# A two-branch attention with a two-layer projection on one core: the first batch in one pass of two streams, weight staging moved, loads by halves

## The chip, the cores and the metric

The kernel runs on one core of a Trainium2 chip. The metric is device time in microseconds (us) of one execution; smaller is better. The core has TensorE (matmuls; PE in the profile, its weight loads PEld), VectorE (DVE), ScalarE (ACT), GpSimd (POOL) and SyncE (SP), whose queue issues all DMAs of this kernel. Each engine works through its own queue in order; semaphores tie them together.

## The reference

```
q, k, v: [8 batches, 8 heads, 576, 64] f32
q_d, k_d, v_d = means over groups of 4 positions            # 144 positions
out_up  = repeat(softmax(q_d k_d^T / 8) v_d, 4)             # each row 4 times
out_loc = softmax(q k^T / 8 where |i - j| < 4) v            # 7 keys a row
x = out_up + out_loc, as [4608 tokens, 512]
h = x @ w_in                                                # [4608, 2048]
out = max(0.01 h, h) @ w_out                                # [4608, 512]
```

The weights `w_in` [512, 2048] and `w_out` [2048, 512] arrive as 64-bit floats; on the chip their bits are turned into a high and a low 32-bit part.

## The kernel before

*Projection.* The tokens are columns. They are cut into chunks of columns; for a chunk of n columns and each of 16 slices f of the hidden width, TensorE does 12 matmuls into a bank `hp` (`up_proj`, L698: 4 slices c of the input times 3 terms, high x high, high x low, low x high), ScalarE and VectorE make `gh` and `gl` out of it (`leaky`, L708 to L711), and TensorE does 12 matmuls into four banks `acc` (`down_proj`, L738: 4 slices e of the output, 3 terms). `store` copies the banks out.

*Chunks and passes.* Batch 0 is two chunks, 256 and 320 columns. They go through the first 8 slices f each, then through the last 8 each (`PASSES`). The partial result of the first half is written to the output in DRAM, fetched back (`refetch`) and added (L763). The other seven batches are cut into 63 blocks of 64 columns; `SIZES` groups these into chunks of 4, 5 and nine times 6 blocks. Inside a chunk a segment is up to 4 blocks of one batch.

*Batch 0* makes its local attention with matmuls on 64-row windows (`banded`, L453 to L521), in two halves of 256 and 320 columns; the averaged branch is `pooled` (L338 to L407), one call for each of four pairs of heads c. `L514` adds both, L519 and L521 split the sum into `xh` and `xl`, the input of the projection.

*The other batches* make the averaged branch with `pooled` too. In it VectorE sums q and k by fours (L338), TensorE multiplies (L351: for each third of the queries one 64-row matmul per head of the pair), softmax follows, the result is transposed (L390), multiplied with the summed v (L380, L402) and copied (L407). The local branch goes over GpSimd: `scores` multiplies q by its 7 neighbouring k (L560), VectorE sums (L566); `values` multiplies by v (L621), VectorE sums (L627); `landing` transposes the result on TensorE (L658), adds the repeated averages (L665) and splits it (L671, L673). The loads of q, k and v hold both heads of a pair, one buffer each.

*Weights.* `convert(f, k)` loads a raw slice of `w_in` (k = 0) or `w_out` (k = 1), 524 KB, into a staging place, converts it with one operation of ScalarE (L266), one of VectorE (L268), one copy (L276 or L279) and one subtraction on GpSimd (L281), and frees the place. Staging places are the buffers k, v, two `prod`, `up`, and for f < 4 also `xh1` and `xl1`. Slices f >= 9 have their final places in memory that is free only when the start's pool `su` is closed (`swap`, signal "late").

*Order.* All this is written as generators that ask a planner, `Order`, for buffers and for engine time. Each has a rank (batch 0: 1 to 5 and its second half 21; weights 20 + 2f + k; other batches from 98 up). The planner keeps a clock for each engine with estimated costs (`COST`), always takes the operation that can start first (then the lowest rank), and so fixes each engine's instruction order before the run. Its estimates give no times here; they only make the order.

Of the kernel before, what the change touches and what calls it, by code (L numbers as in the profile page):

```python
# [27 lines left out]
MAXSEG = 4  # L28
SIZES = (4, 5, 6, 6, 6, 6, 6, 6, 6, 6, 6)
# [4 lines left out]
BLKS = ((0, 4), (4, 9))  # L34
HALFS = 4
HEADS = 2
HF = NF // 2
# [3 lines left out]
def plan():  # L41

    chunks, at = [(0, 256, ()), (256, 320, ())], S
    parts = {b: [] for b in range(BANDED, B)}
    g = 0
    for i, n in enumerate(SIZES):
        mine, z = [], g + n
        while g < z:
            b, j = divmod(g, BLK)
            room = min(BLK - j, z - g)  # L50
            m = -(-room // -(-room // MAXSEG))
            mine.append((b + BANDED, j, j + m, (g - z + n) * NBLK))
            parts[b + BANDED].append((i + 2, j, j + m, (g - z + n) * NBLK))
            g += m
        chunks.append((at, n * NBLK, tuple(mine)))
        at += n * NBLK
    assert g == (B - BANDED) * BLK
    return chunks, parts
# [3 lines left out]
PASSES = [(0, 0, HF), (1, 0, HF), (0, HF, NF), (1, HF, NF)] + [(i, 0, NF) for i in range(2, len(CHUNKS))]  # L62
# [9 lines left out]
LANDED = [NC, NC] + [2 * sum(len(pieces(a, z)) for _, a, z, _ in c[2]) for c in CHUNKS[2:]]  # L72
XMAX = [max(c[1] for c in CHUNKS[i::2]) for i in range(2)]
OMAX = max(XMAX)
COST = {"ACT": (0.13, 0.00083), "DVE": (0.08, 0.00104), "POOL": (0.25, 0.00217)}
HOP = 0.2
SAFE = 0.4
# [18 lines left out]
class Order:  # L96
# [51 lines left out]
    def run(self):  # L148
        while self.tasks:
# [5 lines left out]
            else:  # L155
                best = None
                for task in self.tasks:
                    if task[3][0] == "op":
# [4 lines left out]
                        key = (start, task[0], task[1])  # L163
                        if best is None or key < best[0]:
                            best = key, task
                assert best is not None, [t[3] for t in self.tasks]
# [14 lines left out]
def attn_moe(ctx: ExitStack, tc, qkt, vd, qb, kb, vb, vwb, band, identb, w_in, w_out, ident, edge, out):  # L181
# [5 lines left out]

    bufs = dict(head=HEADS, qk=1, vs=1, qk_d=2, v_d=1, su_vd=2, su_half=1, st_d=2, pd=2, ptd=1, outd=2, q=1, k=1, v=1, s=3, st_l=3, prod=2, up=1,
                xloc=2, lst=3, gh=3, gl=3, o=2, hp=2, pt=2, xh0=1, xl0=1, xh1=1, xl1=1, acc0=1, acc1=1, acc2=1, acc3=1,
# [34 lines left out]
    w_in_v = w_in.rearrange("(c p) (f m) -> p f c m", p=128, m=128 * HALFS)  # L224
    w_out_v = w_out.rearrange("(f p) e -> p f e", p=128)

# [12 lines left out]
    def weight_tiles(pool, f0, f1):  # L239
        shape = [128, f1 - f0, NC, 128]  # L240
        wts.append((f0, *(pool.tile(shape, F32R, name=f"{nm}_{f0}") for nm in ("wih", "wil", "woh", "wol"))))

    def weight(f, k):
        f0, *ts = max((w for w in wts if w[0] <= f), key=lambda w: w[0])
        return ts[2 * k][:, f - f0], ts[2 * k + 1][:, f - f0]

    weight_tiles(const, 0, FSPLIT)

# [3 lines left out]

    def convert(f, k):
        s = yield from slot("k", "v", "prod", "up", *(("xh1", "xl1") if f < 4 else ()))
        st = sb(s, [128, HALFS * (DM + 1)], U16)
        raw = st[:, 1:1 + HALFS * DM]
        if k == 0:
            t = yield from load(raw.rearrange("p (c m) -> p c m", c=NC), w_in_v[:, f], 524e3, s.t)
        else:
            t = yield from load(raw, w_out_v[:, f], 524e3, s.t)  # L260
        mid = st.bitcast(I32).rearrange("p (m w) -> p m w", w=2)[:, :DM, 1]
        top = st.rearrange("p (m h) -> p m h", h=HALFS)[:, 1:, 0].bitcast(BF16)
        s_u = yield from slot("head")
        head = heads[s_u.index % len(heads)]
        t = yield from op("ACT", 1500, t, s_u.t)
# [5 lines left out]
        if f >= FSPLIT:  # L271
            yield from wait("late")
        hi, lo = (w.rearrange("p c m -> p (c m)") for w in weight(f, k))
# [8 lines left out]
        s.free(t)  # L282
        od.signal(("w", f, k), t)
# [12 lines left out]
    def x_tile(i):  # L296
        if i > 1:
            yield from wait(("xbuf", i - 1))
        elif i:
            yield from wait(("scored", 0, NC - 1))  # L300
        s_h, s_l = (yield from slot(f"xh{i % 2}")), (yield from slot(f"xl{i % 2}"))
        xt[i] = [sb(t, [128, NC, XMAX[i % 2]], F32R)[:, :, :CHUNKS[i][1]] for t in (s_h, s_l)]
        od.signal(("xbuf", i), max(s_h.t, s_l.t))
        t = yield from wait(("done", i), 2 if i < 2 else 1)
        s_h.free(t)
        s_l.free(t)

    def fetch(b, c, pool):
        if pool is None:
            sq, sv = (yield from slot(*(("qk", "up") if b < BANDED else ("qk",)))), (yield from slot("vs"))  # L310
            qk, vs = sb(sq, [128, 2, S], F32), sb(sv, [72, 2, 2, D, FAC], F32)
        else:
            sq, sv = None, (yield from slot("su_vs"))
            qk = pool.tile([128, 2, S], F32, name=f"qk{c}")
            vs = sb(sv, [72, 2, 2, D, FAC], F32, pool)
# [4 lines left out]
        tv = yield from load(vs, vd[b, c], 295e3, sv.t if sv else 0.0)  # L320
        return sq, sv, qk, vs, tq, tv

    def pooled(b, c, rank, pool=None):
        sq, sv, qk, vs, tq, tv = yield from fetch(b, c, pool)
        s_qd = yield from slot("qk_d")
        qk_d = sb(s_qd, [128, 2 * SD], F32)
        qkr = qk.rearrange("p a (s r) -> p (a s) r", r=FAC)
        if b < BANDED and (b, c) != (0, 0):
            s = yield from slot("su_half")
            half = sb(s, [128, 2 * SD, 2], F32, pool)  # L330
# [550 lines left out]
```

## Time and profile before

| what | value |
|---|---|
| runs | 976.35, 972.04, 976.05 us; median 976.05 |
| profiled execution | span 965.5 us from first to last instruction; its own total time is not given apart |
| TensorE busy | 936.8 us (97%), 6282 matmuls |
| GpSimd, VectorE, ScalarE busy | 611.5, 594.7, 415.6 us |
| moved by DMA | 117.31 MB, mean 122 GB/s |

In rows of the profile, "out<-in" names tiles by the program's names, "xN" counts instructions, and what stands in brackets or after the bar is the idle time of the engine ahead of them and what ended it. A row of a timeline begins with start and length in us. A stretch row gives the busy time of each engine in it with the number of instructions, then the granted TensorE clock as a share of full speed, the DMA share and GB/s. A row of waits gives the total, the number of times and the longest.

### The profile page before, as it was taken

Reading aid. Unit: us, or ns where it says so; the run is one execution under the profiler, and the core shown is the slowest. Engines: PE = TensorE matmul, PEld = TensorE weight load, DVE = VectorE, ACT = ScalarE, POOL = GpSimd, SP = SyncE. Lnnn points to the kernel's source line nnn. Section 1 sums busy time; section 2 is a strip of 40 time slices with the busy share of each in tenths; the row PEclk is TensorE's granted clock in tenths of the full one; section 3 lists DMA queues with packets and bytes.
Section 4 is the critical chain, followed back from the end, with each engine's and each line's share of the span. In section 5 each row is a group of like instructions: output and inputs, shape, how many; then the busy total and the mean of one; then the engine's idle time right before and its main releaser. Section 6 shows DMA issues by size and latency. Waiting matters only on the chain.

```text
span 965.5 us, 16163 instructions
## 1 busy us (share of the span) xinstructions
PE 936.8 (97%) x6282; PEld 897.8 (93%) x6282; DVE 594.7 (62%) x895; ACT 415.6 (43%) x1139; POOL 611.5 (63%) x356
## 2 busy tenths in 40 slices
PE   6699999899999999999999999999999999999997
PEld 4499999799999999999999899999999999999997
DVE  5897778767876786687667883872753752411111
ACT  3777655434634454345524552532422423422211
POOL 3655766777989788897889785884685783200000
PEclk9689999999999999999999999999999999999999
DMA  9857656434542543446233542351233221000000
GB/s 261 249 189 238 211 175 196 145 121 136 191 128 87 187 141 105 128 152 188 91 115 115 189 150 96 98 154 60 75 90 99 91 62 46 34 1 1 33 1 33
DMA packets 63180, 117.31 MB, mean 122 GB/s; under 512 B 4944, under 2 KB 32848, under 8 KB 63104
## 3 DMA queue, kind: packets, MB, share of 16 engines
q1 hardware_dynamic: 63104, 116.29, 38.6%
q8 instruction: 49, 0.80, 0.3%
q14 instruction: 27, 0.22, 0.1%
HBM read 105.65 MB, written 10.62 MB: 120 GB/s over the span
## 4 chain that ended last, share of the span: by engine, by line
PE 79%; DMA 8%; POOL 7%; DVE 3%; issue 2%; SPq 1%; ACT 0%; POOLq 0%; DVEq 0%; ACTq 0%
PE hp L698 36%; PE acc L738 35%; POOL prod L560 4%; DMA k<-in_kb_dram 3%; POOL prod L621 2%; PE pt L351 2%; DMA qk<-in_qkt_dram 2%; PE pt L390 2%; PE pt L402 1%; DMA v<-in_w_out_dram 1%; PE pt L658 1%; DMA out_dram<-o 1%; DMA su_vw<-in_vwb_dram 1%; DVE s L566 1%; DMA v<-in_vb_dram 1%
## 5 line engine op out<-in xcount | busy, mean ns | idle before, releaser
L560 POOL TENSOR_TENSOR prod<-q,k 128x1344 f32<-128x1344 f32 (+1 forms) x88 | 260.2, 2958 | 93.3 <-DMA k<-in_kb_dram 61.4
L698 PE MATMUL hp<-xh,wih 128*128 128x384 f32 (+2 forms) x832 | 278.7, 335 | 5.1 <-DVE gl L711 5.0
L621 POOL TENSOR_TENSOR prod<-v,s 128x1344 f32<-128x1344 f32 (+1 forms) x88 | 265.3, 3017 | 25.4 <-DVE xloc L627 16.0
L738 PE MATMUL acc<-gh,woh 128*128 128x384 f32 (+2 forms) x832 | 274.8, 330 | 0.6 <-DVE o L763 0.2
L698 PE MATMUL hp<-xl,wih 128*128 128x384 f32 (+2 forms) x832 | 269.5, 324 | 0.0
L698 PE MATMUL hp<-xh,wil 128*128 128x384 f32 (+2 forms) x832 | 269.4, 324 | 0.0
L738 PE MATMUL acc<-gh,wol 128*128 128x384 f32 (+2 forms) x832 | 269.4, 324 | 0.0
L738 PE MATMUL acc<-gl,woh 128*128 128x384 f32 (+2 forms) x832 | 269.4, 324 | 0.0
L708 ACT ACTIVATE gh<-hp 128x384 fp32r<-128x384 f32 (+2 forms) x208 | 97.3, 468 | 318.2 <-PE acc L738 303.6
L711 DVE TENSOR_TENSOR gl<-hp,gh 128x384 fp32r<-128x384 f32 (+2 forms) x208 | 108.3, 522 | 200.4 <-ACT hp L709 198.3
L698 PEld LDWEIGHTS hp<-xh,wih 128*128 128x128 f32 x832 | 157.1, 189 | 13.6 <-DVE gl L711 7.0
L738 PEld LDWEIGHTS acc<-gh,woh 128*128 128x128 f32 x832 | 156.3, 188 | 3.8 <-issue 2.2
L698 PEld LDWEIGHTS hp<-xl,wih 128*128 128x128 f32 x832 | 157.3, 189 | 0.0
L698 PEld LDWEIGHTS hp<-xh,wil 128*128 128x128 f32 x832 | 157.0, 189 | 0.0
L738 PEld LDWEIGHTS acc<-gl,woh 128*128 128x128 f32 x832 | 156.5, 188 | 0.0
L738 PEld LDWEIGHTS acc<-gh,wol 128*128 128x128 f32 x832 | 156.2, 188 | 0.0
L566 DVE TENSOR_REDUCE s<-prod 128x21 f32<-128x1344 f32 (+1 forms) x88 | 130.5, 1483 | 33.1 <-POOL prod L560 33.0
L627 DVE TENSOR_REDUCE xloc<-prod 128x192 f32<-128x1344 f32 (+1 forms) x88 | 130.3, 1481 | 30.1 <-POOL prod L621 29.8
L709 ACT ACTIVATE hp<-hp 128x384 f32<-128x384 f32 (+2 forms) x208 | 96.4, 463 | 0.0
L665 DVE TENSOR_TENSOR pt<-pt,up 128x384 f32<-128x384 f32 (+1 forms) x44 | 38.1, 865 | 31.7 <-PE pt L658 29.0
L645 ACT COPY up<-outd 128x576 f32<-128x576 f32 x84 | 52.3, 675 | 0.0
L338 DVE TENSOR_REDUCE qk_d<-qk 128x288 f32<-128x1152 f32 x29 | 39.0, 1346 | 13.6 <-DMA qk<-in_qkt_dram 13.6
(111 smaller groups left out, 748.9 us busy)
## 6 DMA issues: line engine op xcount, KB each, us to landing
k<-in_kb_dram SPq DMA_DIRECT2D x38, 576.0 KB
v<-in_vb_dram SPq DMA_DIRECT2D x38, 576.0 KB
qk<-in_qkt_dram SPq DMA_DIRECT2D x32, 576.0 KB
vs<-in_vd_dram SPq DMA_DIRECT2D x28, 288.0 KB
q<-in_qb_dram SPq DMA_DIRECT2D x38, 192.0 KB
out_dram<-o SPq DMA_DIRECT2D x36, 192.0 KB
prod<-in_w_out_dram SPq DMA_DIRECT2D x8, 512.0 KB
k<-in_w_in_dram SPq DMA_DIRECT2D x4, 512.0 KB
```

The source lines that it names most:

```text
L338: nc.vector.tensor_reduce(out=qk_d, in_=qkr, axis=AX.X, op=ALU.add)
L560: nc.gpsimd.tensor_tensor(out=prv, in0=q[:, p, a - j0:z - j0].unsqueeze(2).to_broadcast([128, n, W, D]), in1=view(k[:, p], (a - j0) * D, [ ...
L566: nc.vector.tensor_reduce(out=s[:, p, a - j0:z - j0], in_=prv, axis=AX.X, op=ALU.add)
L621: nc.gpsimd.tensor_tensor(out=prv, in0=view(v[:, p], a - j0, [[1, n], [nv, D], [1, W]]), in1=s[:, p, a - j0:z - j0].unsqueeze(2).to_broadc ...
L627: nc.vector.tensor_reduce(out=xl_t[:, :n, p], in_=prv, axis=AX.X, op=ALU.add)
L645: nc.scalar.copy(out=up[:, pp], in_=outd[b][:, 2 * u + pp].unsqueeze(2).to_broadcast([128, SD, FAC]))
L665: nc.vector.tensor_tensor(out=xv, in0=xv, in1=upv, op=ALU.add)
L698: nc.tensor.matmul(hp[:, :n], wt[:, c], x[:, c], start=k == 0, stop=k == 3 * NC - 1)
L708: nc.scalar.activation(out=gh[:, :n], in_=hp[:, :n], func=AF.Prelu, alpha=0.01)
L709: nc.scalar.activation(out=hp[:, :n], in_=hp[:, :n], func=AF.Prelu, alpha=0.01)
L711: nc.vector.tensor_tensor(out=gl[:, :n], in0=hp[:, :n], in1=gh[:, :n].bitcast(F32), op=ALU.subtract)
L738: nc.tensor.matmul(acc[:, :n], wt[:, es], g[:, :n], start=f == f0 and j == 0, stop=f == f1 - 1 and j == 2)
```

## The change

- Batch 0: 512 of its 576 columns are one chunk with four full banks; two streams of 256 columns (`TOP`) go through all 16 slices, the second 8 slices behind the first (`STEPS`). Nothing is written out between. The other 64 columns wait in `rest` (`over`) and open the next chunk, with 3 blocks of batch 1; ten chunks of 6 blocks follow. Segments have at most 3 blocks.
- Weights: the staging places are three parts of the tile `x1` (the odd chunks' input, not yet in use), two `prod` and `up` for f < 9, and for 10 <= f < 14 four more in memory that later holds the last two slices (`stage2`, signal "last"). Loads of f > 9 wait for "late". `w_in` is laid out by slices on the host.
- q, k, v of the local branch are loaded by halves (one head of the pair each) into two buffers each; v sums are a generator of their own (`vsums`), in two halves for batches 1 to 7.
- Batches 1 to 7: q is summed into a block-diagonal tile `qblk`, so L351 becomes one 128-row matmul for each third. Two pairs of heads share one bank and one copy at L402 and L407.
- The planner: an operation may be passed over for one of a rank lower by 5 or more that can start within 0.4 us (GpSimd 0.6). DMA is planned at 265 instead of 300 bytes per ns.

```diff
-MAXSEG = 4
-SIZES = (4, 5, 6, 6, 6, 6, 6, 6, 6, 6, 6)
+MAXSEG = 3
+SIZES = (3,) + (6,) * 10
...
+TOP = [(0, 256), (256, 512)]
+STEPS = [(0, *TOP[0], f) for f in range(LEAD)]
+for f in range(NF):
+    STEPS += [(0, *TOP[1], f)] + [(0, *TOP[0], f + LEAD)] * (f + LEAD < NF)
...
+                if eng in AHEAD and not size:
+                    end = best[0][0] + min(dur, AHEAD[eng])
+                    best = min((o for o in ops if o[1][3][1] == eng and not o[1][3][4] and o[0][0] < end
+                                and o[0][1] <= best[0][1] - (GAP if o[0] != best[0] else 0)),
+                               key=lambda o: (o[0][0] if o[0][1] > best[0][1] - GAP else o[0][0] - 100, o[0][1:]))
...
-                    self.wire = max(self.wire, start + 1.2) + size / 300e3
+                    self.wire = max(self.wire, start + 1.2) + size / 265e3
...
+    def cleared():
+        yield from wait(("x", 0, 0), NC)
+        for t in qblks:
+            nc.gpsimd.memset(t[:, :384], 0)
+            od.signal("cleared", (yield from op("POOL", 200, 0.0)))
...
+    def staging():
+        s_x = yield from slot("x1")
+        stage.append(sb(s_x, [128, bufs["stage"], HALFS * DM], U16))
+        od.signal("stage")
+        s_x.free((yield from wait("converted", 2 * NF)))
     def convert(f, k):
-        s = yield from slot("k", "v", "prod", "up", *(("xh1", "xl1") if f < 4 else ()))
+        if f > FSPLIT:
+            yield from wait("late")
+        s = yield from slot(*(("prod", "up") if f < FREE else ("stage2",) if FSPLIT < f < LSPLIT else ()), "stage")
...
+        if b >= BANDED:
+            yield from wait("cleared", len(qblks))
...
+            nc.vector.tensor_reduce(out=k_d, in_=qk[:, 1].rearrange("p (s r) -> p s r", r=FAC), axis=AX.X, op=ALU.add)
+            for p in range(2):
+                rows = slice(64 * p, 64 * p + 64)
+                t = yield from op("DVE", 576, t)
+                nc.vector.tensor_reduce(out=q_d[rows, :, 64 * p:64 * p + QB],
+                                        in_=qk[rows, 0].rearrange("p (a s r) -> p a s r", a=3, r=FAC), axis=AX.X, op=ALU.add)
...
+            if b >= BANDED:
+                nc.tensor.matmul(sc[:, qi * SD:(qi + 1) * SD], q_d[:, qi], k_d, start=True, stop=True)
+                continue
...
+        if b >= BANDED:
+            if c % 2 == 0:
+                halves[b, c] = mine[0]
+                od.signal(("half", b, c))
+                return
+            yield from wait(("half", b, c - 1))
+            mine.insert(0, halves.pop((b, c - 1)))
...
-        s_q, s_k = (yield from slot("q")), (yield from slot("k"))
-        q, k = sb(s_q, [128, 2, MAXSEG, D], F32), sb(s_k, [128, 2, MAXSEG + W - 1, D], F32)
...
+        for p in range(2):
+            s_q, s_k = (yield from slot("q")), (yield from slot("k"))
+            q, k = sb(s_q, [128, MAXSEG, D], F32), sb(s_k, [128, MAXSEG + W - 1, D], F32)
...
+                    nc.tensor.matmul(acc[:, a:z], w[h][:, es], g[:, :n], start=(a, f, j) == (0, 0, 0),
+                                     stop=f == NF - 1 and j == 2, skip_group_check=ch == 0)
```

More of the change, by code (lines that the diff above doesn't have):

```diff
@@ L271, in convert @@
         if f >= FSPLIT:
-            yield from wait("late")
-        hi, lo = (w.rearrange("p c m -> p (c m)") for w in weight(f, k))
+            yield from wait("late" if f < LSPLIT else "last")
+        lo, hi = weight(f, k)
         if k:
@@ L319, in fetch, with vsums @@
         od.signal(("qk", b, c), tq)
-        tv = yield from load(vs, vd[b, c], 295e3, sv.t if sv else 0.0)
-        return sq, sv, qk, vs, tq, tv
+        return sq, qk, tq
+    vds = {}
+    def vsums(b, c, pool=None):
+        yield from wait(("asked", b, c))
+        s_vd = None
+        for p0, p1 in (((0, 2),) if pool else ((0, 1), (1, 2))):
+            sv = yield from slot("su_vs" if pool else "vs")
+            vs = sb(sv, [72, p1 - p0, 2, D, FAC], F32, pool)
+            tv = yield from load(vs, vd[b, c, :, p0:p1], 147e3 * (p1 - p0), sv.t)
+            if s_vd is None:
+                s_vd = yield from slot("su_vd" if pool else "v_d")
+                v_d = sb(s_vd, [72, 2, 2, D], F32, pool)
+            t = yield from op("DVE", 512 * (p1 - p0), tv, s_vd.t)
+            nc.vector.tensor_reduce(out=v_d[:, p0:p1], in_=vs, axis=AX.X, op=ALU.add)
+            sv.free(t)
+        vds[b, c] = s_vd, v_d
+        od.signal(("vd", b, c), t)
@@ L376, in pooled @@
         s_st.free(t)
-        s_vd = yield from slot("su_vd" if pool else "v_d")
-        v_d = sb(s_vd, [72, 2, 2, D], F32, pool)
-        td = yield from op("DVE", 1050, tv, s_vd.t)
-        nc.vector.tensor_reduce(out=v_d, in_=vs, axis=AX.X, op=ALU.add)
-        if sv:
-            sv.free(td)
         s_pt = yield from slot("ptd")
@@ new lines, in values @@
+        (a, z), = pieces(j0, j1)
+        yield from wait(("turn", ORD[b, j0, u]))
+        s_x = yield from slot("xloc")
+        od.signal(("turn", ORD[b, j0, u] + 1))
+        xl_t = sb(s_x, [128, 3, 2, D], F32)
+        for p in range(2):
+            s_v, v, tv = got[p]
+            s_p = yield from slot("prod")
+            pr = sb(s_p, [128, 3 * W * D], F32)
+            prv = pr[:, :nj * W * D].rearrange("p (j d t) -> p j d t", j=nj, d=D)
+            tp = yield from op("POOL", nj * W * D, ts, tv, s_p.t)
+            nc.gpsimd.tensor_tensor(
+                out=prv,
+                in0=view(v, 0, [[1, nj], [nv, D], [1, W]]),
+                in1=s[:, p, :nj].unsqueeze(2).to_broadcast([128, nj, D, W]),
+                op=ALU.mult)
+            t = yield from op("DVE", nj * W * D, tp, s_x.t)
+            nc.vector.tensor_reduce(out=xl_t[:, :nj, p], in_=prv, axis=AX.X, op=ALU.add)
+            s_p.free(t)
+            s_v.free(tp)
@@ L742, in down_proj @@
+                if f == NF - 1 and last:
+                    od.spawn(-5, store(ch, e, s_a, acc, t))
             s_g.free(t)
             s_l.free(t)
-    def dest(p, e, n):
-        base = CHUNKS[PASSES[p][0]][0]
-        return out[e * 128:(e + 1) * 128, base:base + n]
-    def refetch(p, e, n):
-        s_o = yield from slot("o")
-        o = sb(s_o, [128, OMAX], F32)
-        tw = yield from wait(("half", PASSES[p][0]), 4)
-        t = yield from load(o[:, :n], dest(p, e, n), 512 * n, s_o.t, tw)
-        reload[p, e] = s_o, o
-        od.signal(("reload", p, e), t)
@@ L757, in store @@
-    def store(p, e, n, s_a, acc, t):
-        key, f0, f1 = PASSES[p]
-        if f0 > 0:
-            tr = yield from wait(("reload", p, e))
-            s_o, o = reload.pop((p, e))
-            t = yield from op("DVE", n, t, tr)
-            nc.vector.tensor_tensor(out=o[:, :n], in0=acc[:, :n], in1=o[:, :n], op=ALU.add)
-        else:
+    def store(ch, e, s_a, acc, t):
+        base, n = CHUNKS[ch][:2]
+        cuts = TOP if ch == 0 else [(0, n)]
+        for a, z in cuts:
             s_o = yield from slot("o")
```

334 lines of the change are left out of this document (176 added, 158 removed).

## The prediction

> **What bounds the kernel now.** I read the page first (busy shares), then the stretches of the run, then who TensorE waits for, then the order of single instructions at the start.
>
> ```profile
> span 965.5 us, 16163 instructions
> ...
> PE 936.8 (97%) x6282; PEld 897.8 (93%) x6282; DVE 594.7 (62%) x895; ACT 415.6 (43%) x1139; POOL 611.5 (63%) x356
> ```
>
> ```profile
> core 0: us, PE busy (x) PEld busy (x) DVE busy (x) ACT busy (x) POOL busy (x), PEclk, DMA share, GB/s
> 5.00:48.50 43.50, 32.58 (x312) 22.73 (x312) 31.65 (x67) 25.43 (x79) 24.20 (x23) 0.80 0.92 262
> 48.50:56.00 7.50, 7.50 (x67) 6.73 (x65) 7.29 (x13) 4.51 (x11) 3.72 (x4) 0.57 0.55 165
> 56.00:140.00 84.00, 83.31 (x723) 78.40 (x721) 63.72 (x103) 57.24 (x153) 53.70 (x37) 1.00 0.67 211
> 140.00:250.00 110.00, 103.61 (x844) 98.04 (x844) 83.32 (x142) 51.01 (x164) 82.06 (x52) 1.00 0.49 153
> 640.00:950.00 310.00, 310.00 (x1795) 308.76 (x1793) 119.14 (x166) 94.18 (x221) 125.40 (x68) 1.00 0.16 50
> ```
>
> TensorE is the bound from 56 us on. It is not fully used in two places only: the start (up to 56 us, lower granted clock too) and the ramp from 140 to 250 us, 6.4 us short. A busy share can hide slow issue, so I price its main work by the spacing of matmuls in an undisturbed stretch of the chain.
>
> ```profile
> 69.84 2.86 PE hp L698 x24
> 101.31 3.52 PE hp L698 x24
> 858.03 4.19 PE hp L698 x24
> ```
> ```profile
> L698 PE MATMUL hp<-xh,wih 128*128 128x384 f32 x576 | 198.1, 344 | 0.5 <-DVE gl L711 0.5
> L698 PE MATMUL hp<-xh,wih 128*128 128x320 f32 x128 | 41.4, 323 | 0.1
> L698 PE MATMUL hp<-xh,wih 128*128 128x256 f32 x128 | 39.2, 306 | 4.5 <-DVE gl L711 4.5
> ```
>
> Each form stands for six kinds of the same count (three terms for hp, three for acc), so there are 576 x 6 / 24 = 144 groups of 24 at 4.19 us, 32 at 3.52 and 32 at 2.86: 603.4 + 112.6 + 91.5 = 807.5 us. The rest of the 965.5, 158 us, is the start, the attention's small matmuls and waits.
>
> ```profile
> PE hp L698 <- DVE gl L711: 5.0, 6, 2.8
> PE pt L402 <- DVE xl L673: 1.3, 1, 1.3
> PE pt L351 <- DVE qk_d L338: 0.9, 2, 0.5
> PE acc L738 <- DVE o L763: 0.2, 1, 0.2
> PE acc L738 <- ACT o L772: 0.2, 1, 0.2
> ```
>
> These are all of TensorE's waits after 56 us: 7.6 us. So a change that leaves the matmuls as they are can win 7.6 us after the start, and whatever it takes off the start.
>
> **The change, part by part.** *New chunks.* 256 + 320 and 256 + 320 + nine of 384 columns become 512 (as two streams of 256), 256 and ten of 384. That is 160 groups at 4.19 and 48 at 2.86: 670.4 + 137.3 = 807.7 us. Term: 0. The first batch's partial results no longer go to DRAM and back (8 reloads, 8 stores and 8 additions fewer); TensorE waited 0.2 us for that. Term: 0.
>
> *The start.* The first projection needs the first half of batch 0 for all four head pairs.
>
> ```profile
> 27.41 0.91 POOL L371 TENSOR_TENSOR pd<-pd,st_d 128x432 f32<-128x432 f32 x1 [0.89 <-PE pt L390]
> ```
> ```profile
> 36.44 1.35 DVE L338 TENSOR_REDUCE qk_d<-qk 128x288 f32<-128x1152 f32 x1 [2.57 <-DMA qk<-in_qkt_dram]
> 37.71 0.42 DVE L514 TENSOR_TENSOR acc<-acc,outd 128x256 f32<-128x256 f32 x1
> 44.10 0.97 DVE L268 SCALAR_TENSOR_TENSOR k<-k,head 128x512 int32<-128x512 int32 x1
> 45.11 0.88 DVE L276 CAST woh<-k 128x512 fp32r<-128x512 f32 x1
> 46.19 0.41 DVE L514 TENSOR_TENSOR acc<-acc,outd 128x256 f32<-128x256 f32 x1
> 49.37 0.41 DVE L521 TENSOR_TENSOR xl<-acc,xh 128x256 fp32r<-128x256 f32 x1
> ```
> ```profile
> 40.17 1.24 PE L402 MATMUL pt<-ptd,su_vd 72*64 72x144 f32 x8 [2.52 <-DVE xloc L469]
> 53.06 0.58 PE L698 MATMUL hp<-xh,wih 128*128 128x256 f32 x1
> ```
>
> At 33.9 us VectorE, whose queue is in order, stops 2.57 us for batch 1's q and k and then sums them for 1.35 us, while batch 0's L514 and L469 stand behind; L402 on TensorE waits 2.52 us for L469. In the new kernel batch 1's sums wait for "cleared", which waits for all four x of the first half, so this block of 3.9 us cannot come back. (Its v sums are not held; they are half as long as a load and come with rank 98.) Later L268 and L276, weight conversions, hold the last head pair's L514 for 1.85 us; the look-ahead (rank 4 against 20 and more) should put L514 first. I take 6 us for both. Bounds: 0, if another wait steps in; and 13: from L371's 27.41 to L521's end at 49.8 are 22 us, in which this head pair needs eight steps (L390, L392, L402, L407, L502, L514, L519, L521); at 0.4 to 1.24 us as in these rows, about 1 us with the handover, that is 8 to 9.
>
> *Block-diagonal q.* Per head pair of batches 1 to 7, six 64-row matmuls become three of 128 rows; 28 pairs.
>
> ```profile
> 140.07 0.34 PE L351 MATMUL pt<-qk_d 64*64 64x144 f32 x2 [0.40 <-DVE qk_d L338]
> 140.07 0.46 PE L351 MATMUL pt<-qk_d 64*64 64x144 f32 x4 [0.40 <-DVE qk_d L338]
> 140.07 0.95 PE L351 MATMUL pt<-qk_d 64*64 64x144 f32 x12 [0.40 <-DVE qk_d L338]
> 140.96 0.41 PE L698 MATMUL hp<-xh,wih 128*128 128x320 f32 x1
> 141.21 0.31 PE L698 MATMUL hp<-xl,wih 128*128 128x320 f32 x1
> ```
>
> The first three rows are one burst, cut off 0.13 and 0.23 us after its start, and whole. Twelve records (two per matmul) take 0.89 us until L698 starts. Counting records one would halve that and win 0.44 x 28 = 12.5 us. But the records come two at a time: the end moves by 0.12 us for two more, and 0.12 x 6 pairs is 0.72 of the 0.89. The upper and the lower 64 rows run side by side already. Three full matmuls have six records; one per 0.12 us, they end as before, less the second's offset inside a pair. I take 0.05 us a pair, 1.5 us; bounds 0 and 3.
>
> The Trainium skill, "TensorE: Matmul & The Clock Gate", Part 3 (Packing small matmuls), says that matmuls on different row groups overlap, a packed set costing one matmul plus about 4 ns per further tile. By that rule the block form brings 0 and the sum would be 965.0. The trace agrees: 0.12 us per pair.
>
> For this form VectorE does three sums of 576 elements each for one of 1152 (1.35 us above). At half its elements plus a fixed part (an estimate) each takes 0.75, 2.2 in all: +0.9 x 28 = 25 us of VectorE; the v sums in two parts add a little. VectorE would be busy 620 of 953 us. Cover: its 38% idle time. Gone, it would cost those 25 us, most of it in the ramp (83.3 of 110 busy). Term: 0.
>
> *Two head pairs share one bank and one copy of the averages.* 14 bursts fewer on TensorE. After a burst the first L698 is 0.25 us ahead of the second, not 3.52 / 24 = 0.15, and 0.89 - 0.72 = 0.17 us go by before it: up to 0.27 each. I take half, 14 x 0.14 = 2 us; bounds 0 and 3.8.
>
> *The ramp: q, k, v by halves in two buffers, segments of at most three blocks.* GpSimd's products stay the same in number of elements, so its total doesn't shrink.
>
> ```profile
> POOL prod L560 <- DMA k<-in_kb_dram: 14.8, 8, 3.1
> ```
> ```profile
> 111.93 1.30 POOL L281 TENSOR_TENSOR wol<-up,woh 128x512 fp32r<-128x512 f32 x1 [0.36 <-DVE woh L276]
> 113.28 2.11 POOL L560 TENSOR_TENSOR prod<-q,k 128x896 f32<-128x896 f32 x1
> ```
>
> From 113 to 260 us GpSimd waits 14.8 us for k. Today one buffer holds both halves, so the next load is issued after the second product; with two, the next first half loads during the second product. Also k, v and, after weight 8, the product buffers no longer stage weights, so products can start before 113. The new chunk after the first batch needs two segments, not two of four blocks. So most of the 7.6 us of waits should go: I take 5; bounds 0 and 7.2. On SP's queue the loads are twice as many and half as large, 0.33 us an issue in the next fence. The copies into two buffers cost no engine. What is late next is TensorE itself.
>
> *Weights and the look-ahead.* Loads of weight 10 and up now wait until the start's pool is released; before, only their last conversion step did.
>
> ```profile
> L502 PE MATMUL pt<-su_pt,su_vs x80: 222/222/369, 50.0 to 78.4; 70*64 70x64 f32 x80
> ```
> ```profile
> 102.78 0.33 SPq L216 DMA_DIRECT2D up<-in_w_out_dram  x1
> 81.99 3.52 PE hp L698 x24
> ```
>
> The pool's last reader starts at 78.4; with L514 to L521 behind it, release is near 79.7. From load issue to the end of the subtraction the last weight took 102.78 to 113.2: 10.5 us, so weight 10 is ready at about 90. The second stream begins at 82.0 today; 6 us earlier is 76, and weight 10 is five steps of 2.86 and about 12% of small work later: 92. Margin 2 us. After that weights come from seven staging places, two per 6.2 us being wanted. I put +2 us for waits here and for engines held up to 0.6 us by the look-ahead; bounds 0 and +8.
>
> **Sum.** -6 - 1.5 - 2 - 5 + 2 = -12.5 us: span 953. Around the span lay 976.05 - 965.5 = 10.55 us if the profiled execution was like the median (6.5 if like the fastest of the three runs shown). Time: 963.5.
>
> **Rivals.**
> (A) The forecast, about 957 to 970.
> (B) The start doesn't move: L402 and L502 of the last head pair find another wait (a product bank, a late weight on ScalarE). For: L371 and L402 above wait for different engines, and batch 1's v sums can stop VectorE as its q and k did. Against: the look-ahead puts batch 0 first. -6.5: 969.5.
> (C) Nothing is won: the start as in B and new waits as large as the ramp's. 976.
> (D) The head pairs run through almost without waits: -13 at the start, -7 in the ramp, -3.5 for the bursts, no new wait: 952.5. Against: a half-clock start (0.57 granted in the second row above) slows whatever is there.
> (E) Slower: the startup pool is released late and TensorE stands at weight 10. Price: release + 10.5 - 92. To eat 14.5 us and add 4.9, release must come after 101 us, 21 later than today. For: the second half of batch 0 has the rank of weight 0 and competes with an earlier projection. Against: the look-ahead prefers it to weights from 3 on. From 981 up, 985 at 25 us later.
>
> **How the numbers follow.** A 0.50, B 0.20, C 0.12, D 0.10, E 0.08. A difference of 0.5% (4.9 us) is about what a measurement here can tell from none: below 971.2 fall A but for 0.05, two thirds of B, and D: 0.68; above 980.9 lie E and 0.02 of C: 0.10; between them 0.22. The range 948 to 980 takes in A, B, D and most of C and leaves out E.
>
> **What would show it.** The start: first full run of L698 at about 47 us, no L338 among batch 0's operations on VectorE. Block form: L351 with half the records and about the same 0.85 us a burst; a burst of 0.5 would prove me wrong. Ramp: TensorE's waits after 56 us below 3 us, k waits on GpSimd under 5 us up to 260. Weights: no gap at L698 between 76 and 115 us; one there means E. The stretch of matmuls near the end stays at 4.19 per 24; if not, the whole sum is wrong.

## The result, and the profile after

The changed kernel takes 944.84 us (944.16 to 946.09), the kernel before 974.82 us (972.04 to 976.35) in the same series: ratio 0.971, 95% interval 0.9679 to 0.9741. The forecast, 963.5 us, had the right direction; the time lies 3 us below its range.

The page of the changed kernel, and who TensorE waits for after 56 us (total, times, longest):

```profile
span 944.3 us, 16161 instructions
...
PE 917.2 (97%) x6114; PEld 893.5 (95%) x6114; DVE 619.0 (66%) x960; ACT 413.9 (44%) x1128; POOL 611.8 (65%) x349
```
```profile
PE hp L793 <- POOL wil L308: 3.1, 2, 2.6
PE hp L793 <- DVE gl L806: 1.9, 3, 1.5
PE acc L828 <- ACT o L846: 1.4, 2, 0.9
PE hp L793 <- ACT wih L306: 1.4, 1, 1.4
PE acc L828 <- DVE gl L806: 1.3, 2, 1.0
PE pt L407 <- DVE qblk L380: 0.9, 1, 0.9
```

L793 and L828 are the projection (L698 and L738 before), L407 the scores (L351), L444, L468 and L755 the other small matmuls of the attention (L390, L402, L658). This execution took 946.09 us, so 1.8 us lie around its span. The waits did not go: they are 10.0 us instead of 7.6, and 4.5 us of them, the rows of `wil` and `wih`, wait for weights, which is new. So the 21.2 us by which the span is shorter must come from elsewhere. Stretches of the run, columns as before:

```profile
5.00:39.00 34.00, 27.58 (x274) 19.17 (x274) 20.87 (x48) 18.52 (x62) 15.26 (x17) 1.00 0.87 245
...
56.00:140.00 84.00, 76.48 (x646) 73.50 (x646) 79.60 (x117) 51.39 (x137) 68.74 (x42) 0.98 0.63 209
140.00:250.00 110.00, 108.39 (x864) 105.97 (x863) 101.53 (x164) 61.42 (x192) 101.30 (x56) 1.00 0.56 171
```

The ramp (140 to 250 us) is filled, 108.39 instead of 103.61 us busy, and VectorE and GpSimd stand at 101 of 110 us there. The weight phase (56 to 140) has lost: 76.48 instead of 83.31. The granted clock of 1.00 in the first row is not to be believed: the trace's record of the clock begins at 28.2 us only, and the transposes with `id_sb` took 0.42 to 0.43 us until 24.2 us and 0.27 to 0.30 from 29.4 us on. In the kernel before the record begins at 20.8 us, with the same lengths on either side, so the 0.80 from 5.00 to 48.50 us there is too high as well.

To place the 21.2 us I used the start of every matmul in both traces. The undisturbed distance of two projection matmuls of n columns is n/2400 + 0.0135 us (24 x 0.1735 = 4.16 us at 384, as in the chain near the end of the changed kernel). What a distance has above that is called a *wait* if no other matmul lies between, and the *cost of a burst* if small matmuls do. So a wait here also holds what slows the matmuls themselves, such as a lower clock, and the sums are larger than those of the rows above. The undisturbed projection is 804.7 us in both kernels.

| us | before | after | difference | forecast |
|---|---|---|---|---|
| by 56 us: time less projection done | 53.1 | 46.0 | -7.1 | -6 |
| waits, 56 to 140 | 1.9 | 11.2 | +9.3 | +2 (weights) |
| waits, 140 to 250 | 7.0 | 2.5 | -4.5 | -5 (ramp) |
| waits, after 250 | 13.3 | 7.9 | -5.4 | 0 |
| bursts of small matmuls after 56 | 79.3 | 66.9 | -12.4 | -3.5 |

Before rounding they add up to -20.0; 1.2 us of the 21.2 lie in the edges between parts.

Most of the fourth row is not waiting. The prediction's row at 858.03 has 4.19 us for 24 matmuls of the kernel before; the chain of the changed kernel has, at the same place:

```profile
862.51 4.16 PE hp L793 x24
```

From 250 us on, 384-column matmuls that follow one another start 174.7 ns apart on average before and 173.4 ns after (distances from 50 ns above 173.5 up left out). Over some 3200 of them that is 4 of the 5.4 us. All runs below that are built on the kernel before have 174.2 to 174.8 ns, all that are built on the changed kernel 173.4 to 173.5. So the difference comes with a part that no experiment took out (the streams and chunks, the staging, or where the tiles lie in memory); which of them it is stays open.

### The profile page after: what moved, and what is told of

It reads as the page before. It is cut to its first block, busy times and chain, and to the rows that moved or that the text cites. A ratio compares the mean times of both kernels' runs of the same rounds, so it can differ in the third digit from the quotient of the medians.

```text
span 944.3 us, 16161 instructions
## 1 busy us (share of the span) xinstructions
PE 917.2 (97%) x6114; PEld 893.5 (95%) x6114; DVE 619.0 (66%) x960; ACT 413.9 (44%) x1128; POOL 611.8 (65%) x349
## 4 chain that ended last, share of the span: by engine, by line
PE 90%; DVE 4%; ACT 2%; DMA 2%; issue 1%; POOL 1%; SPq 0%; DVEq 0%; ACTq 0%; POOLq 0%
PE hp L793 41%; PE acc L828 40%; PE pt L444 2%; PE pt L407 2%; PE pt L468 2%; PE pt L755 1%; DVE x L295 1%; DMA su_vs<-in_vd_dram 1%; DMA out_dram<-o 1%; ACT head L293 1%; DVE woh L303 1%; PE pt L558 0%; PE acc L411 0%; POOL prod L657 0%; SPq L231 0%
## 5 line engine op out<-in xcount | busy, mean ns | idle before, releaser
L793 PE MATMUL hp<-x,wih 128*128 128x384 f32 (+1 forms) x1664 | 406.5, 329 | 3.4 <-DVE gl L806 1.9
L657 POOL TENSOR_TENSOR prod<-q,k 128x1344 f32<-128x1344 f32 x84 | 261.3, 3110 | 81.4 <-DVE xloc L724 68.9
L793 PEld LDWEIGHTS hp<-x,wih 128*128 128x128 f32 x1664 | 287.4, 189 | 6.1 <-DVE gl L806 2.5
L718 POOL TENSOR_TENSOR prod<-v,s 128x1344 f32<-128x1344 f32 x84 | 262.4, 3128 | 21.4 <-DVE xloc L724 21.1
L828 PE MATMUL acc<-gh,woh 128*128 128x384 f32 (+1 forms) x832 | 273.6, 329 | 1.6 <-ACT o L846 1.4
L793 PE MATMUL hp<-x,wil 128*128 128x384 f32 (+1 forms) x832 | 269.8, 324 | 3.1 <-POOL wil L308 3.1
L828 PE MATMUL acc<-gl,woh 128*128 128x384 f32 (+1 forms) x832 | 269.0, 323 | 1.3 <-DVE gl L806 1.3
L828 PE MATMUL acc<-gh,wol 128*128 128x384 f32 (+1 forms) x832 | 268.9, 323 | 0.0
L793 PEld LDWEIGHTS hp<-x,wil 128*128 128x128 f32 x832 | 157.1, 189 | 3.5 <-POOL wil L308 3.5
L828 PEld LDWEIGHTS acc<-gh,woh 128*128 128x128 f32 x832 | 156.5, 188 | 3.2 <-ACT o L846 2.5
L828 PEld LDWEIGHTS acc<-gl,woh 128*128 128x128 f32 x832 | 156.6, 188 | 1.7 <-DVE gl L806 1.7
L828 PEld LDWEIGHTS acc<-gh,wol 128*128 128x128 f32 x832 | 156.4, 188 | 0.0
L663 DVE TENSOR_REDUCE s<-prod 128x21 f32<-128x1344 f32 x84 | 129.4, 1541 | 7.3 <-POOL prod L657 7.3
L724 DVE TENSOR_REDUCE xloc<-prod 128x192 f32<-128x1344 f32 x84 | 129.4, 1541 | 5.4 <-POOL prod L718 5.3
L380 DVE TENSOR_REDUCE qblk<-qk 64x144 f32<-64x576 f32 x56 | 41.4, 740 | 0.8
```

What stands on the lines that cost most here:

```text
L380: nc.vector.tensor_reduce(out=q_d[rows, :, 64 * p:64 * p + QB], in_=qk[rows, 0].rearrange("p (a s r) -> p a s r", a=3, r=FAC), axis=AX.X, ...
L657: nc.gpsimd.tensor_tensor(out=prv, in0=q[:, a - j0:z - j0].unsqueeze(2).to_broadcast([128, n, W, D]), in1=view(k, (a - j0) * D, [[D, n], [ ...
L663: nc.vector.tensor_reduce(out=s[:, p, a - j0:z - j0], in_=prv, axis=AX.X, op=ALU.add)
L718: nc.gpsimd.tensor_tensor(out=prv, in0=view(v, 0, [[1, nj], [nv, D], [1, W]]), in1=s[:, p, :nj].unsqueeze(2).to_broadcast([128, nj, D, W]) ...
L724: nc.vector.tensor_reduce(out=xl_t[:, :nj, p], in_=prv, axis=AX.X, op=ALU.add)
L793: nc.tensor.matmul(hp[:, :n], w[h][:, ws], x[:, c], start=k == 0, stop=k == 3 * NC - 1)
```

## The experiments

The changed kernel itself ran in the first series only. Each experiment ran in one of four later series beside the kernel before, whose median there was 974.3 us (one, four, six, ten), 974.2 (five, seven, eight, thirteen), 972.6 (the second hold of five, eleven, twelve) and 969.8 (two, three, nine). A difference to 944.84 us is therefore one between series and can be off by some us; ratios compare within a series. Code is shortened in the cuts.

**One. The scores as 64-row matmuls again.** All else is as changed, the operands come from the block-diagonal tile.

```diff
-nc.tensor.matmul(sc[:, cols], q_d[:, qi], k_d, ...)
+for r in (0:64, 64:128): nc.tensor.matmul(sc[r, cols], q_d[r, qi, r], k_d[r], ...)
```

> The new kernel with the block tile and all other instructions in the same order, only L407 as six 64-row matmuls instead of three of 128 rows. Theory D (a change between 64-row and 128-row use of the array costs TensorE a pause at each burst): L407's bursts last 0.88 us instead of 0.64, the first L793 after them is 0.05 us slower as well, so 28 x 0.24 to 0.29 = 7 to 8 us more: about 952. Rival P (as predicted: pairs overlap, nothing else): 28 x 0.05 = 1.5 us more: about 946. Rival H (TensorE's gain there is hidden by other waits): the bursts differ but the time stays at 945.

Measured: 953.44 us, ratio 0.9789 (0.9752 to 0.9826), 8.6 us slower than with the block form (7.7 by the ratios). VectorE, ScalarE and GpSimd do the same operations in the same order here and in experiments two and three, so nothing but the matmuls differs. One burst in the timeline of the changed kernel, then of this one (start, length; the rows ahead and behind are projection):

```profile
160.69 0.28 PE L793 MATMUL hp<-x,wil 128*128 128x256 f32 x1
160.81 0.90 PE L407 MATMUL pt<-qblk 128*128 128x144 f32 x6
161.45 0.49 PE L793 MATMUL hp<-x,wih 128*128 128x256 f32 x2
```
```profile
161.72 0.28 PE L793 MATMUL hp<-x,wil 128*128 128x256 f32 x1
161.92 0.95 PE L407 MATMUL pt<-qblk 64*64 64x144 f32 x12
162.81 0.50 PE L793 MATMUL hp<-x,wih 128*128 128x256 f32 x2
```

From the last projection matmul ahead to the first behind it is 0.76 us in one, 1.09 in the other. The pairs of 64-row matmuls do run side by side, as forecast: 12 records are hardly longer than 6 (0.95 and 0.90 us). But TensorE stands where the form of the array changes: the first score comes 0.20 us after the matmul ahead of it instead of 0.12, and behind the last one there is another pause. Over all bursts that hold scores alone (26 in each trace) the cost is 1.04 us with 64 rows and 0.65 with 128; in the kernel before it was 1.01 (16 such bursts). All bursts together cost 7.8 us more here than in the changed kernel.

**Two and three. Count or form?** The two forms also differ in the number of matmuls. So one matmul more was put ahead of each pair's three, in one form or the other.

```diff
+if qi == 0: nc.tensor.matmul(sc[:, :SD], q_d[:, 0], k_d, ...)                # two
+if qi == 0: nc.tensor.matmul(sc[:64, :SD], q_d[:64, 0, :64], k_d[:64], ...)  # three
```

> The changed kernel with its first score matmul of each of the 28 pairs of batches 1 to 7 issued twice, in the same form of 128 rows (same output columns, so the result stays). Theory F (a change of the array form costs a pause): no change of form is added, so only two records of 0.122 us for each pair, 28 x 0.244 = 6.8 us: about 951.5 us; the bursts get longer by 0.24 us a pair, the 0.028 us between the last small matmul and the next projection matmul stays. Theory G (the bursts' cost is a fixed price for each instruction or each burst, the form does not matter): the same here.

> The same, but the extra matmul ahead of each pair's three has 64 rows and 64 columns of queries (rows 0 to 63 of the block tile; its result is written over by the next). Theory F: beside the two records, each of the extra matmuls brings a change into the 64-row form and one out of it, about 0.10 + 0.19 us: 28 x 0.29 = 8.1 us more than with the extra 128-row matmul, about 959.5 us. Theory G: no more than with the 128-row one, about 951.5 us or less.

Measured: 951.98 us (ratio 0.98, 0.9761 to 0.9839) and 960.51 us (0.9876, 0.9833 to 0.9919): 7.1 us above the changed kernel for the matmul itself (7.1 by the bursts of the traces too, 8.8 by the ratios), and 8.5 us more for its form; these two ran in one series. The same burst in the two:

```profile
161.22 0.28 PE L794 MATMUL hp<-x,wil 128*128 128x256 f32 x1
161.34 0.41 PE L407 MATMUL pt<-qblk 128*128 128x144 f32 x2
161.58 0.90 PE L408 MATMUL pt<-qblk 128*128 128x144 f32 x6
162.22 0.38 PE L794 MATMUL hp<-x,wih 128*128 128x256 f32 x1
```
```profile
161.63 0.28 PE L794 MATMUL hp<-x,wil 128*128 128x256 f32 x1
161.84 0.46 PE L407 MATMUL pt<-qblk 64*64 64x144 f32 x2
162.23 1.00 PE L408 MATMUL pt<-qblk 128*128 128x144 f32 x6
162.97 0.49 PE L794 MATMUL hp<-x,wih 128*128 128x256 f32 x2
```

The second starts 0.21 us after the matmul ahead instead of 0.12, the block's first 0.39 us later instead of 0.24, and that group lasts 0.74 us to the next projection instead of 0.64: 0.09 us on the way into the 64-row form and 0.25 behind it. From projection to projection it is 1.34 against 1.00 us. Theory F holds: the pause belongs to the change of form. (Whether TensorE empties itself in it or waits for weights to be loaded is not to be seen.) The Trainium skill, "TensorEngine Tiling (Array Packing)", section Tiling Modes, Key Properties, states that changing the tiling mode drains TensorE; the trace agrees as far as a pause stands at each change, and gives about 0.3 us for a burst.

**Four. One bank and one copy for each pair** (the branch that joins two pairs taken out).

```diff
-if b >= BANDED:      # join pairs c and c + 1
+if False:
```

> The new kernel with one bank and one copy for each head pair at L468 again (28 bursts of 8 records instead of 14 of 16). Theory D: each burst saved is worth its pause of 0.2 us before the next L793 and 0.1 us in it, 14 x 0.25 = 3.5 us more: about 948. Rival P: 14 x 0.14 = 2 us more: 947. If the plan's new order matters more than that, the time leaves 944 to 950.

Measured: 950.41 us, ratio 0.976 (0.9724 to 0.9797), above the 944 to 950 expected. A burst of L468 alone costs 0.74 us for one pair here and 1.27 for two in the changed kernel, so 14 joins save 14 x (2 x 0.74 - 1.27) = 2.9 us of TensorE. The rest of the 5.6 us goes with a wait that has grown:

```profile
PE acc L828 <- ACT o L846: 5.6, 4, 2.7
```

It was 1.4 us in the changed kernel; ScalarE has 14 copies more to do. The plan's order is another one too, and no run separates the two.

**Five. The products held back until the weights are done.** The first local branch waits for all 32 converted slices.

```diff
+yield from wait("converted", 2 * NF)     # ahead of the local branch
```

> The new kernel, but no segment of the local branch (its loads, L657, L718) is planned before all 32 weight slices are converted. In the new kernel's trace VectorE's conversions L295 and L303, 0.68 and 0.41 us when GpSimd is idle, took 3.50, 2.57 and 2.60 us where one of GpSimd's 3.1 us products L657 ran, and TensorE waited 7.8 us between 56 and 140 us. Theory C (products among the conversions hold VectorE up and so TensorE): no conversion over 1.9 us, TensorE's waits between 56 and 140 us at most 3 us; the time 938 to 943 if GpSimd catches up, since it is idle later. Rival W (weight 10 comes late because its load waits for the release of the start's pool): the waits at L793 near 87 to 90 us stay at 3 us or more, time 944 to 950.

Measured: 944.7 us, ratio 0.9709 (0.9677 to 0.9741): no change in time, where theory C expected 938 to 943, but the cause of the weight waits shows. In the changed kernel's timelines of VectorE and GpSimd:

```profile
71.05 3.50 DVE L295 SCALAR_TENSOR_TENSOR x<-x,head 128x512 int32<-128x512 int32 x1
```
```profile
70.91 3.10 POOL L657 TENSOR_TENSOR prod<-q,k 128x1344 f32<-128x1344 f32 x1
```

The conversion ends with the product beside it, 0.54 us after its end; the same operation takes 0.68 at 85.20. The range of the 17 on tile `x` (minimum, median and maximum in ns), in the changed kernel and with the products held back:

```profile
L295 DVE SCALAR_TENSOR_TENSOR x<-x,head x17: 651/1124/3504, 37.6 to 116.0; 128x512 int32<-128x512 int32 x17
```
```profile
L295 DVE SCALAR_TENSOR_TENSOR x<-x,head x17: 652/927/1805, 34.6 to 108.9; 128x512 int32<-128x512 int32 x17
```

Not every VectorE operation suffers: the sum L663 takes 1.54 us at 80.08 beside GpSimd's L308 and keeps a mean of 1541 ns over all 84. But it is not the second input alone that decides, for the cast L303 has one input, takes 0.41 us at 64.27 and here waits out a product that ends at 108.61:

```profile
106.29 2.60 DVE L303 CAST woh<-x 128x512 fp32r<-128x512 f32 x1
```

The Trainium skill, "GPSIMD Engine Reference", section Specifications, states that the SBUF interfaces are shared with VectorE, with contention for its instructions that have two inputs in SBUF or run in a 2-port performance mode. L295 has two inputs in SBUF; the trace agrees, with 3.50 for 0.68 us. Whether L303 ran in such a mode no run here shows.

With the products held back no conversion L295 takes over 1.81 us, and the waits from 56 to 140 us fall from 11.2 to 6.4 us (by rows of waits as above from 7.5 to 4.2, where theory C expected 3 at most), those for the weight halves from 4.5 to 0.6. The hold takes two things away at once, VectorE's slow conversions and the products ahead of L308 in GpSimd's own queue, and no run separates them; but ahead of the L308 at 86.30 us GpSimd stood idle for 1.57 us until VectorE's L303, so there VectorE was the late one. Then the waits come back: 15.3 instead of 9.5 us from 140 to 620; that the late products are the cause is argued, not tested. A hold until 26 slices are converted does the same:

> The new kernel with the local branch held until 26 of 32 weight slices are converted (e5: all 32, no difference in time). If the early products' cost to VectorE's conversions and their gain for the ramp balance, a middle start takes some of both: 940 to 943. If the end is set by the sum of TensorE's work and the order of the rest, it stays at 944 to 947.

Measured: 944.76 us, ratio 0.9717 (0.969 to 0.9745). The waits are 7.9 us from 56 to 140 and 13.5 from there to 620. Neither hold is better than the changed kernel.

**Six. The look-ahead off** (`AHEAD = {}`).

> The new kernel planned without the look-ahead. Theory S (the look-ahead puts batch 0 ahead of weight work and so starts the projection 8 us earlier): first L793 at 45 us or later instead of 39.9, time 4 to 7 us more: 949 to 952. Rival G (the start moved because batch 1's sums can no longer block VectorE, and because of buffers): first L793 stays at 40 to 42, time 944 to 947.

Measured: 950.53 us, ratio 0.9762 (0.9725 to 0.98). The first projection matmul comes at 44.7 us instead of 39.9 (36.8 to 37.5 in experiments one to three, with the changed kernel's order). Stretches of the start: the kernel before, the changed one, and this one (the last three numbers are granted clock, DMA share, GB/s):

```profile
30.00:45.00 15.00, 10.27 (x91) 6.92 (x91) 12.29 (x22) 8.78 (x24) 9.18 (x8) 0.53 0.92 270
45.00:55.00 10.00, 9.24 (x82) 7.76 (x83) 9.04 (x16) 6.54 (x17) 6.30 (x5) 0.50 0.37 115
```
```profile
30.00:45.00 15.00, 13.08 (x155) 9.70 (x155) 13.15 (x31) 12.36 (x36) 10.12 (x10) 1.00 0.61 207
45.00:55.00 10.00, 10.00 (x137) 9.10 (x136) 9.35 (x19) 8.60 (x21) 7.42 (x6) 1.00 0.69 223
```
```profile
30.00:45.00 15.00, 11.33 (x105) 7.66 (x106) 14.61 (x24) 9.65 (x25) 12.37 (x10) 0.61 0.69 220
```

In the kernel before the record has the clock at 1.00 from 20.8 us, at 0.50 from 31.0 and at 1.00 again from 54.9; with the look-ahead off it is at 0.50 from 33.3 to 47.0; in the changed kernel at 1.00 from 28.2 to 89.6. In the 3.4 us ahead of the two falls TensorE was busy for 49% and 67%. So where the projection starts late it also starts at half clock. That the gaps set off the fall is read from these traces; no run tests it alone.

**Seven. DMA planned at 300 again** (`size / 300e3`).

> The new kernel planned with DMA at 300 bytes per ns again instead of 265. Theory M (the slower figure fits the 245 to 262 GB/s that the start moves, so the plan puts fewer operations ahead of data that is late): first L793 later than 42 us, time 947 to 951. Rival: the look-ahead and the gate carry the start alone, time within 2 us of 945.

Measured: 950.54 us, ratio 0.9771 (0.9741 to 0.9801). The time is in the 947 to 951 that theory M expected, but the start is not later (37.4 us), so its reason falls; the waits for ScalarE's copies are 5.8 us (`o`, L846) and those for `gl` 5.8. The constant shifts the order, and no single place explains the 5.7 us. An order that is merely another one can thus cost this much, which bears on every experiment here that lets the planner plan anew (four to twelve).

**Eight. q and k loaded whole,** one buffer each (v still in halves).

```diff
-for p in range(2):
-    q, k = sb(s_q, [128, MAXSEG, D], F32), ...     # two buffers each
+q, k = sb(s_q, [128, 2, MAXSEG, D], F32), ...      # one buffer each
```

> The new kernel with q and k loaded for both heads at once into one buffer each, as before (v stays in halves). Theory R (two half buffers took the waits for k out of the ramp): GpSimd waits 10 to 15 us for k between 113 and 260 us instead of 3, TensorE's waits after 140 us grow by 3 to 5 us, time 948 to 950. Rival N: with products started at 71 us and segments of 3 blocks GpSimd has slack, TensorE waits no more, time within 2 us of 945.

Measured: 955.3 us, ratio 0.982 (0.979 to 0.985), the largest loss of any one part undone, and more than theory R's 948 to 950; but GpSimd's waits for k were 5.1 us in 113 to 260, not the 10 to 15 expected. It was this, on TensorE and on VectorE:

```profile
175.31 0.97 PE L407 MATMUL pt<-qblk 128*128 128x144 f32 x6 [0.36 <-DVE qblk L380]
180.50 1.68 PE L444 MATMUL pt<-id_sb,pd 128*72 128x128 f32 x6 [4.21 <-ACT pd L435]
```
```profile
177.04 0.16 DVE L420 TENSOR_SCALAR st_d<-pt 128x3 f32<-128x3 f32 x1
177.12 0.55 DVE L766 TENSOR_TENSOR x<-pt,x 128x384 fp32r<-128x384 f32 x1
177.59 1.54 DVE L720 TENSOR_REDUCE xloc<-prod 128x192 f32<-128x1344 f32 x1
179.05 0.67 DVE L360 TENSOR_REDUCE v_d<-vs 72x128 f32<-72x512 f32 x1
179.64 0.15 DVE L426 TENSOR_SCALAR st_d<-pt 128x3 f32<-128x3 f32 x1
```

The softmax's L426 stands behind L720 and L360 in VectorE's order, ScalarE's L435 waits for it, and TensorE for that. Bursts from 140 to 250, which hold this hole, cost 24.0 instead of 16.3 us, waits 6.2 instead of 2.5. Not all of that is waiting, for behind the hole the clock is at half for 10.2 us:

```profile
180.70:190.90 10.20, 9.45 (x47) 8.05 (x47) 6.57 (x9) 3.60 (x12) 10.20 (x6) 0.50 0.81 268
```

TensorE was busy 9.45 us there; at full clock up to half of that, 4.7 us, would not have been needed (an estimate). So this one hole of 4.21 us can cost about the same again by the clock.

**Nine. Whole loads and 64-row scores together.**

> The changed kernel with q and k loaded whole into one buffer each and also the six 64-row matmuls from the block tile. Theory S (both cost TensorE time of their own): 944.8 + 10.5 + 8.6 = 963.9 us. Theory I (with whole loads GpSimd, VectorE and their handover set the pace, so TensorE's small work is partly free): 955 to 958 us.

Measured: 960.99 us, ratio 0.9882 (0.9846 to 0.9918); against 0.982 that is 0.6%, some 6 us for the form, with intervals of 0.3% on either side. The traces are clearer: bursts after 56 us cost 7.0 us more than in experiment eight. So theory I falls, and S holds for the larger part: most of the block form's gain does not hang on the half loads.

**Ten to twelve. The kernel before with parts of the change.** First the gate alone (sums of q and k of batches 1 to 7 after batch 0's four x), then the block tile with it, then also look-ahead and 265.

```diff
+yield from (wait(("x", 0), NC) if b >= BANDED else ())
```

> The kernel before, with one wait added in the plan: batches 1 to 7 don't sum q and k before all four head pairs of batch 0's first half have delivered x. Theory G (3.9 us of VectorE's queue were lost at 33.9 us to batch 1): first L698 at 44 to 45 us instead of 48.5, time 3 to 5 us less than before. Rival S: another wait steps in, first L698 later than 47, time within 1.5 us of before.

> The kernel before with the wait of e4 (batch 1's sums after batch 0's first half) and the block-diagonal q of the new kernel; all else as before. Theory D (a change between 64-row and 128-row use of the array costs TensorE a pause at each burst): L407's counterpart lasts 0.64 us instead of 0.88, the first matmul behind it is as much slower as behind the transposes, so 7 to 8 us less than e4's 963.7: about 956. Rival P: 1.5 us less: 962. Rival V (VectorE, which has 25 us more to do for this form, becomes the bound in the ramp): more waits of TensorE between 140 and 250 us, time 960 to 966.

> e9 with the look-ahead and the planned DMA rate of 265 added; batch 0 is still two chunks in two passes, with whole loads and the old staging. Theory A (the order is worth about 6 us each way, as undoing the look-ahead and the rate cost 5.7 each in the new kernel): first L698 at 42 us or earlier, time 946 to 951; the two streams, the staging and the half loads then carry 5 us at most. Rival B (they carry the rest of the gain): time 953 to 958.

Measured: 963.67 us (ratio 0.9891, 0.9857 to 0.9925); 964.46 us (0.9925, 0.9896 to 0.9954); 965.51 us (0.9921, 0.9886 to 0.9955). The gate brings about 1.1%, more than the 3 to 5 us expected: the first projection matmul comes 2.1 us earlier and the waits of 140 to 250 fall from 7.0 to 3.6 us. Profile against profile it is 3.8 us (spans of 961.7 and 965.5); the rest is about what the median of the kernel before lies above its profiled execution. The block form added to it makes the bursts of scores cheaper as above (0.98 to 0.65 us), and the time does not fall; it stays in the 960 to 966 of rival V. In the profiled execution the waits after 56 us rise from 20.2 to 43.1 us, led by these of TensorE and of GpSimd (the latter from 113 to 260 us):

```profile
PE hp L722 <- DVE gl L735: 13.7, 16, 3.0
```
```profile
POOL prod L584 <- DMA k<-in_kb_dram: 20.5, 9, 6.0
```

That execution (span 971.8 us) is slower than its median, so the size is not to be read from it. With the planner's part the projection starts at 41.6 us, as theory A expected, but the time is above both ranges (946 to 951 and 953 to 958): one hole of 10.8 us stands in the ramp (TensorE waits 4.5 us for `qblk`, 3.9 for `st_l`). Where VectorE and GpSimd are behind, time saved on TensorE seems to turn into waiting for them; these two profiles alone show it. What the streams, the staging, the half loads and the joined pairs add to this kernel together is some 20 us; no run takes the streams or the staging alone.

**Thirteen. The kernel before once more,** to look at its spread.

> The kernel before, unchanged. Its profiled span was 965.5 us while its runs have spans of 968 to 978 (time less 1.8). Theory V (what varies is when batch 1's q and k land, for which VectorE's queue stands at the start): a profile of a slower execution shows a longer wait at L338 near 34 us, and the whole difference before 56 us. Rival U: the difference is spread over the run, or lies in the ramp's k loads.

Measured: 971.81 us (966.55 to 975.08), ratio 0.9975 (0.9946 to 1.0003). Its profiled execution has a span of 971.8 us, 6.3 us longer than the one of the prediction. The theory that VectorE's wait for batch 1's q and k makes the difference falls: it was 1.36 us here and 2.57 there. The difference is spread: the granted clock at 56 to 64 us (0.65 against 1.00), longer waits at 142.9, 249.9, 405.6 and 480.1 us (1.84, 1.33, 0.62 and 0.55 us). What sets it off stays open.

## Why the prediction was wrong

The time is 18.7 us below the forecast: 8.75 us by the base, 8.7 by the sum (12.5 us instead of 21.2), and 1.25 because the changed kernel's profiled execution lies above its median.

*The base.* "Around the span lay 976.05 - 965.5 = 10.55 us" is the first step that failed. 1.8 us lie there, in the changed kernel (946.09 - 944.3) and in later runs of the kernel before (1.8 or 1.9 in nearly all, 2.4 at most); the 6.5 named beside it was too much as well. So the profiled execution took about 967.3 us, 8.75 less than the median. The measured gain is 30 us against the median, 21.2 against that execution; the kernel before varies by 1% and more from one execution to the next, the changed one by 0.2% in its four.

*The block form,* taken at -1.5 us with bounds 0 and 3, is the term that was mis-sized: 8.6 us by undoing it, 10 by its bursts (28 x (1.01 - 0.65)). The step "one per 0.12 us, they end as before" was right for the matmuls and overlooked the pauses around them, 0.09 us on the way into the 64-row form and 0.25 on the way out. The clue stood in the quoted rows: "0.89 - 0.72 = 0.17 us go by before" L698 was read as a cost of any burst, and put to the joining of pairs. It is a cost of the array's form, and goes with it. The rule of Part 3 in "TensorE: Matmul & The Clock Gate" (the Trainium skill) holds inside a set, as the 12 records show; it says nothing of entering and leaving the set. The test "a burst of 0.5 would prove me wrong" was half met: 0.64 in the trace (160.81 to 161.45) where 0.85 was expected.

*The joined pairs:* -2 forecast, -2.9 on TensorE; undone, 5.6 us with the waits for ScalarE.

*The start:* -6 forecast, -7.1 measured, the first projection matmul at 39.9 instead of about 47 us. The mechanism (no sums of batch 1 among batch 0) is borne out: the first L380 is at 66.3 us, and the gate alone moves the start by 2.1 us. But some 3 us of it are the granted clock, which was left as it was: in the rows quoted before, from 48.50 to 56.00, 7.5 us ran at 0.57, and 7.5 x 0.43 = 3.2 us is what full clock saves (an estimate).

*The ramp:* -5 forecast, -4.5 by the waits; k costs GpSimd 3.1 us up to 260 us, under the 5 named. But "TensorE's waits after 56 us below 3 us" failed: 10.0.

*Weights:* +2 forecast, bounds 0 and +8; 9.3 us of new waits from 56 to 140 us, 3.9 of them in the two rows below. The place was right:

```profile
86.66 0.50 PE L793 MATMUL hp<-x,wih 128*128 128x256 f32 x2 [1.36 <-ACT wih L306]
...
89.73 0.58 PE L793 MATMUL hp<-x,wil 128*128 128x256 f32 x1 [2.57 <-POOL wil L308]
```

At their end, at 89.6 us, the clock fell, which nothing in the prediction allowed for; 1.6 us (an estimate: projection matmuls in this stretch at half clock) of the 9.3 are due to it:

```profile
89.60:93.00 3.40, 3.27 (x15) 3.27 (x16) 3.40 (x3) 1.07 (x4) 3.23 (x3) 0.51 0.78 259
```

The waits for weights are where rival E put them, but not for its reason, a late release of the pool: the pool's last reader, L573, starts at 67.0 us, 11 earlier than before. The products among the conversions are, as the fifth experiment shows (4.5 to 0.6 us). "Cover: its 38% idle time" for VectorE was a share of the whole run: where the 25 us fell, from 56 to 250 us, VectorE was busy 181 of 194 us.

*Chunks:* 0 forecast, on the ground that 24 matmuls take 4.19 us in both. They take 4.16 in the changed kernel, so this term, put at nothing, was 160 x 0.03 = 4.8 us (an estimate), most of what the excess after 250 us fell by. The sign "stays at 4.19 per 24; if not, the whole sum is wrong" showed it, though small. The cause stays open.

Rival B and C fall with the start, E with its price. D (the head pairs run through, 952.5) came nearest, by luck: its -13 at the start and its "no new wait" did not come. Undone one at a time the parts cost 8.6, 5.6, 5.7, 5.7 and 10.5 us, 36 in all, more than the whole 30 (34 and 28 by the ratios): they hang on one another, and each new plan has costs of its own, so none of these numbers is a part's share.

## What to carry to other kernels

Price a group of small matmuls by the distance from the last large matmul ahead to the first behind it, not by its own records; where it has another array form than the work around it, the pauses on the way in and out (0.3 us here) can be worth more than what is saved on the matmuls themselves. Before a sum starts from a profiled execution, find out how that execution stands to the median: the time around the span is small, and the rest is spread. A saving on the engine that bounds the kernel counts only where the others are ahead; look at their load in that stretch, not over the run. And after a hole in TensorE's work look at the granted clock before you put the whole loss down to waiting.

## What was not expected of the hardware

- A change of TensorE between 128-row and 64-row matmuls cost about 0.1 us on the way into 64 rows and 0.25 us on the way back to 128 (experiment three against two; 0.33 us for both in experiment one).
- A VectorE operation of 0.68 us took 3.50 us beside a GpSimd product of 3.10 us; a cast with one input took 2.60 us instead of 0.41 beside another; sums with one input did not stretch.
- TensorE busy 9.24 of 10 us (45 to 55 us, before) still had a granted clock of 0.50, while the changed kernel, with 13.08 of 15 us busy ahead of it, kept 1.00. Matmuls last longer at half clock, so the two busy times are not alike.
- Behind a TensorE wait of 4.21 us the clock stayed at 0.50 for 10.2 us (experiment eight), at the end of one of 2.57 us for 3.4 us (the changed kernel); behind one of 2.79 us, at 192.6 us of the kernel before, it did not fall.
